# Sparse attention and a routed expert layer: the first expert's third block computed with tokens held and weights streamed

## Chip, cores and metric

One core of a Trainium2 chip runs the whole program. The metric is device time in microseconds, the median of three runs: 1031.38 us for the kernel before (1029.55 to 1036.73).

## What is computed

Eight batches of eight heads of attention over 576 tokens with head size 64, in which each query keeps its 32 largest scores. Its output is the input `x` (4608 tokens of 512 values) of a layer with eight experts: a token with `x @ w_skip > 0` goes to the one expert with the largest gate value.

```python
scores = scale * np.matmul(q, k.transpose(0, 1, 3, 2))
kth = np.partition(scores, -top_k, axis=-1)[..., -top_k:-top_k + 1]
scores = np.where(scores >= kth, scores, -1000000000.0)
...
for e in range(E):
    mask = e_idx == e
    h = np.maximum(xc[mask] @ w1[e], 0.0)
    y[mask] = gate_w[mask, None] * (h @ w2[e])
out[do_compute] = xc + y
```

## The kernel before

The attention takes the first 779 us of the span, the experts the rest. Only the expert stage matters here, and in it the passage from the first expert to the second.

Tokens are gathered by expert into blocks of 128 (`XG`, at most `NB` = 3 blocks, so `TN` = 384 tokens). A block is turned by four PE transposes into a px buffer (two of these in PSUM), ACT copies it as `XH` (the high part, line 1052), and DVE writes the remainder `XL` (line 1056). Weights are split in the same manner: ACT writes the high part (`part_hi`, line 966), DVE the remainder (`part_lo`, line 969), in four quarters per layer. Every product is then three products of high and low parts.

`up` (lines 1111 to 1118) computes 128 hidden values of all tokens of a stretch: the weights are held in the array, the tokens are streamed, 12 products into a ph buffer (three of these). ACT's relu writes the high part of the hidden values to `HH[f]` (line 1121), DVE the remainder to `HL[f]` (line 1124); f runs over `FC` = 8 groups of 128 hidden values. `down` (lines 1135 to 1141) holds 128 hidden values of a block's 128 tokens and streams 512 columns of the second layer, three products for each f and block, into py, one buffer for each block.

The first expert (e = 0) is computed while the last routing step is still running: its first two blocks (`EARLY` = 2) with ups of 224 tokens (32 to 256) and their downs, then the third block alone, once its tokens are gathered: `upping(EARLY * P, TN, ...)`, eight ups of 128 tokens. These pieces are handed to the planner `pl`, which sorts tasks on each engine by readiness and due times and writes the program order that the engines follow. In the same call the three blocks of the second expert are gathered by POOL and turned (`turning(1, j, ...)`), and the first-layer weights of the second expert are split as soon as the ups that read the old ones are done (`done`). After `pl.run()` the order is that of plain code: the downs of the third block (e = 0), with the splits of the second-layer weights (`ahead_of`) between them, then for e = 1 to 7 eight ups with relus and splits, and the downs with the splits of the next second layer and the turns of the next expert.

Weights come by transfers on SP's queue (`fetch`), tokens by indirect transfers on POOL's queue (line 1029), and sums go back by line 1042.

Of the kernel before, what the change touches and what calls it, by code (L numbers as in the profile page):

```python
# [9 lines left out]
F32 = mybir.dt.float32  # L10
# [3 lines left out]
AF = mybir.ActivationFunctionType  # L14
# [9 lines left out]
EARLY = NBLK - 1  # L24
# [19 lines left out]
def tile_kernel(ctx, tc, q, k, v, w_skip, w_gate, w1, w2, out):  # L44
    nc = tc.nc
# [4 lines left out]
    P = 128  # L50
# [9 lines left out]
    CC = DM // P  # L60
# [29 lines left out]
    identF = cp.tile([P, P], F32, name="identF")  # L90
# [180 lines left out]
    pl = Plan()  # L271
# [19 lines left out]
    for c0, n, src in ((0, E, w_gate), (E, 1, w_skip.rearrange("(f o) -> f o", o=1))):  # L291
        gates.append((GW[:, :, c0:c0 + n], src.rearrange("(c p) e -> p c e", p=P)))
        pairs = src.rearrange("(c u d) e -> u d c e", u=2, d=D)
        for u in range(2):
            c = c0 + (E + 1) * u
# [31 lines left out]
    NB = NBLK  # L327
# [615 lines left out]
    FC = F // P  # L943
    FQ = F // 4
    TN = NB * P
    WHI, WLO = [None] * 2, [None, [None] * 4]
    WRAW = [WA, [WB[:, i] for i in range(4)]]
    XG, XH, XL = [None] * 2, [None] * 2, [None] * 2
# [75 lines left out]
    room_of = lambda e: (TN,) [0] if e == 0 else ROOM[e - 1]  # L1024
# [13 lines left out]
    def finish(xg, j, ix, py):  # L1038
        scatter(summed(xg, j, py), ix)
# [23 lines left out]
    def turning(e, j, bank, due, after):  # L1063

        h = Hold(bank, 2)
        st = {}
        x = pl.add("PE", 0.47, due, lambda: st.__setitem__("v", turned(e, j, h()[:, 0:512])), after, take=h)
        x = pl.add("ACT", 0.48, due, lambda: turned_hi(e, j, st["v"]), x, give=[h])
        return pl.add("DVE", 0.6, due, lambda: turned_lo(e, j, st["v"]), x, give=[h])
# [13 lines left out]
    PARTED = []  # L1083
    FETCHED = {}
    for n in range(16):
        w, i, half = n // 8, n // 2 % 4, n % 2
        FETCHED.setdefault((w, i), []).append(pl.add("SP", 0.63, NR * NP * n // 16 - K["ld"] + K["fe"], lambda w=w, i=i, half=half: fetch(0, w, i, half),
                                                     LOADED[0, NP * n // 16], lag=5.0))
    for i in range(4):
        x = pl.add("ACT", 1.06, D0 + 1 + i, lambda i=i: part_hi(0, i), room, PENNED[NP - 1], FETCHED[0, i])  # L1090
        PARTED.append(pl.add("DVE", 1.22, D0 + 1 + i, lambda i=i: part_lo(0, i), x))
    x = pl.add("DVE", 0.3, D0, lambda: to_index(IDX[0], LS, EB), ROUTED[0])
    y = pl.add("POOL", 1.6, D0, lambda: nc.gpsimd.memset(XG[0], 0.0), room)
    XT = []
    for j in range(EARLY):
        g = pl.add("POOL", 1.1, D0, lambda j=j: gather(XG[0], j, ix(0, j), N - S), x, y, STORED[B - 2], [STORES[p] for p in range(NP - H // 2)], lag=3.0)
# [5 lines left out]
    mp = ms.enter_context(tc.tile_pool(name="mp", bufs=1, reuse_waits="tile"))  # L1102
# [8 lines left out]
    def up(e, f, ph, u, w):  # L1111

        xh, xl = XH[e % 2], XL[e % 2]
        h1, l1 = (a[0][f // 2].rearrange("p (c f) -> p c f", c=CC)[:, :, f % 2 * P:(f % 2 + 1) * P] for a in (WHI, WLO))
        for c in range(CC):
            nc.tensor.matmul(ph[:, u:w], h1[:, c], xh[:, c, u:w], start=(c == 0), stop=False)  # L1116
            nc.tensor.matmul(ph[:, u:w], h1[:, c], xl[:, c, u:w], start=False, stop=False)  # L1117
            nc.tensor.matmul(ph[:, u:w], l1[:, c], xh[:, c, u:w], start=False, stop=(c == CC - 1))  # L1118
# [11 lines left out]
    D1 = D0 + 10  # L1130
# [12 lines left out]
    def upping(u, w, due, after):  # L1143
        r = []
        for f in range(FC):
            h = Hold(PH, 2)
            x = pl.add("PE", 12 * max((w - u) / 2400 + 0.013, 0.107), due + 0.4 * f, lambda f=f, h=h: up(0, f, h(), u, w), PARTED[f // 2], after, take=h)
            y = pl.add("ACT", 0.17 + (w - u) / 1200, due + 0.4 * f, lambda f=f, h=h: relu_hi(f, h.t, u, w), x, give=[h])
            r.append((x, pl.add("DVE", 0.16 + (w - u) / 960, due + 0.4 * f, lambda f=f, h=h: relu_lo(f, h.t, u, w), y, give=[h])))
        return r  # L1150
# [16 lines left out]
    x = pl.add("DVE", 0.35, D1, places, ROUTED[0])  # L1167
    pl.add("DVE", 2.6, D1 + 2, lambda: sort_experts(IDXF, IDX[1]), x)
    g = pl.add("POOL", 1.1, D1, lambda: gather(XG[0], NB - 1, ix(0, NB - 1)), x, STORED[B - 1], STORES[NP - 1], lag=3.0)
    done = upping(EARLY * P, TN, D1 + 12, turning(0, NB - 1, PX, D1 + 8, g))  # L1170
    for j in range(NB):
        g = pl.add("POOL", 1.1, D1 + 1, lambda j=j: gather(XG[1], j, ix(1, j)), x, STORED[B - 1], STORES[NP - 1], lag=3.0)
        turning(1, j, PX, D1 + 12.1 + 0.8 * j, g)
# [91 lines left out]
    check = checks()  # L1265
    for j in range(EARLY):
        finish(XG[0], j, ix(0, j), PY0[j])
    for e in range(E):
        for f in range(FC) if e else ():
            ph = ps_g.tile([P, 512], F32, name="ph", bufs=3)  # L1270
            up(e, f, ph, 0, room_of(e))
            relu_hi(f, ph, 0, room_of(e))
            relu_lo(f, ph, 0, room_of(e))
            ahead_of(e, 0, f)
            if e > 1:
                next(check, None)
        PY = [ps_g.tile([P, 512], F32, name=f"py{j}", bufs=1) for j in range(NB)] if e else PY0
        ots = []
        if e + 1 < E:
            for f in range(FC):  # L1280
                for j in range(blocks_of(e)) if e else (NB - 1,):
                    down(f, j, PY[j])
                    if f == FC - 1:
                        ots.append((summed(XG[e % 2], j, PY[j]), ix(e, j)))
                ahead_of(e, 1, f)
                if e > 1:
                    next(check, None)
                if e and f % 2 and f // 2 < blocks_of(e + 1):
                    turn_x(e + 1, f // 2)
        else:  # L1290

            for j in range(blocks_of(e)):
                for f in range(FC):
                    down(f, j, PY[j])
                finish(XG[e % 2], j, ix(e, j), PY[j])
        if e + 2 < E:
            for j in range(blocks_of(e + 2)):
                gather(XG[e % 2], j, ix(e + 2, j))
        for x in ots:
            scatter(*x)  # L1300
# [210 lines left out]
```

## Time and profile before

| | us |
|---|---|
| median of 3 runs | 1031.38 |
| lowest, highest | 1029.55, 1036.73 |
| the profiled execution | 1031.82 |
| its span, first to last instruction | 1030.0 |
| PE busy | 986.7 (96%) |
| DVE busy | 896.6 (87%) |
| ACT busy | 836.3 (81%) |
| mean granted clock of PE | 0.989 |

The busy shares are means over two stages: in the attention DVE, ACT and POOL are all near 9 tenths, in the last quarter of the span they are mostly between 1 and 7, while PE stands at 9 in nearly every slice. The rows below are of the stretches around the change. A row of a timeline reads: start, time, engine, line, operation, output from inputs, shapes, how many, and in brackets the idle time before it and what ended it. A product's time holds its latency, so two products that follow one another are best read by the distance of their starts.

### The profile page before, as it was taken

What the parts mean: (1) busy time and instruction counts of PE and PEld (TensorE: products, weight loads), DVE (VectorE), ACT (ScalarE), POOL (GpSimd) and SP (SyncE); (2) the same over time, 40 slices, a digit from 0 to 9 for tenths busy, and PEclk for the clock granted to TensorE, in tenths of its full rate; (3) what the DMA queues carried; (4) which work ended last, traced back from release to release, by engine and by line L of the source; (5) the groups of instructions that cost most, each with busy time, mean ns of one, the idle gap of its engine ahead of it and who ended that gap; (6) DMA issues with size and microseconds to landing.
All of it is one profiled execution on the core that took longest, in us unless ns stands there. A gap on an engine that the chain in (4) does not pass through costs nothing.

```text
span 1030.0 us, 38832 instructions
## 1 busy us (share of the span) xinstructions
PE 986.7 (96%) x14632; PEld 700.4 (68%) x14632; DVE 896.6 (87%) x4986; ACT 836.3 (81%) x1485; POOL 706.3 (69%) x864
## 2 busy tenths in 40 slices
PE   8499999999999999999999999999999999999996
PEld 4156666666666666666666565666678889988995
DVE  6989999999999999999999999999986746765661
ACT  6799999999999999999999998999983544433540
POOL 3988899888888888988988988799961212211210
PEclk9799999999999999999999999999999999999998
DMA  5333334343443334434333333333226465554610
GB/s 126 62 87 77 87 76 98 88 103 91 100 97 77 87 90 102 99 73 114 91 88 76 87 82 93 85 86 77 48 50 206 155 215 174 175 157 158 217 66 21
DMA packets 215493, 106.64 MB, mean 104 GB/s; under 512 B 149512, under 2 KB 200712, under 8 KB 215296
## 3 DMA queue, kind: packets, MB, share of 16 engines
q1 hardware_dynamic: 210736, 94.30, 36.0%
q0 software_dynamic: 3360, 9.47, 2.7%
q8 instruction: 117, 1.92, 0.8%
q14 instruction: 80, 0.66, 0.2%
q10 hardware_dynamic: 1200, 0.30, 0.1%
HBM read 76.93 MB, written 24.53 MB: 98 GB/s over the span
## 4 chain that ended last, share of the span: by engine, by line
PE 67%; DVE 22%; ACT 5%; POOL 3%; issue 2%; DMA 1%; POOLq 0%; ACTq 0%
PE r L621 10%; PE r L769 9%; DVE cand L692 8%; DVE cl L721 5%; PE pt L852 5%; PE pa L852 4%; PE ph L1116 4%; PE py L1139 4%; PE ph L1117 4%; PE ph L1118 4%; PE py L1141 4%; PE py L1140 4%; DVE cand L700 3%; PE r L760 3%; DVE cl L698 3%
## 5 line engine op out<-in xcount | busy, mean ns | idle before, releaser
L708 POOL TENSOR_TENSOR xw<-XC,r 128x576 f32<-128x576 f32 x288 | 366.2, 1284 | 49.6 <-ACT r L705 28.7
L692 DVE MAX8 cand<-XC 128x8 f32<-128x82 f32 (+1 forms) x2016 | 364.4, 229 | 9.2 <-ACT XC L649 9.1
L705 ACT ACTIVATE r<-XC,cl 128x576 bf16<-128x576 f32 x288 | 224.9, 785 | 11.5 <-DVE cl L698 8.4
L721 DVE MAX8 cl<-xw 128x8 f32<-128x585 f32 x288 | 215.6, 756 | 3.1 <-POOL xw L712 1.5
L621 PE MATMUL r<-TT 64*64 64x512 f32 (+1 forms) x1280 | 190.3, 416 | 0.8 <-ACT XC L630 0.7
L716 POOL TENSOR_SCALAR PEN<-XC,cl 128x576 bf16<-128x576 f32 x94 | 162.7, 1731 | 24.2 <-DVE cand L700 12.3
L769 PE MATMUL r<-TT 64*128 64x512 f32 (+1 forms) x528 | 148.8, 641 | 12.0 <-ACT XC L651 12.0
L621 PE MATMUL r<-TS 64*64 64x512 f32 (+1 forms) x1024 | 154.3, 416 | 1.4 <-DMA TS<-TT 1.4
L718 ACT ACTIVATE PEN<-XC,cl 128x576 bf16<-128x576 f32 x194 | 150.1, 788 | 3.7 <-DVE cl L721 3.7
L698 DVE MAX8 cl<-cand 128x8 f32<-128x56 f32 (+2 forms) x864 | 151.9, 182 | 0.2
L802 ACT ACTIVATE PTM<-r,tops 128x1024 f32<-128x1024 f32 x124 | 137.6, 1121 | 6.3 <-PE r L760 5.9
L649 ACT ACTIVATE XC<-r 128x1024 f32<-128x1024 f32 x128 | 132.5, 1038 | 4.3 <-PE r L621 4.1
L760 PEld LDWEIGHTS <-PEN 64*128 64x128 bf16 (+1 forms) x2880 | 71.0, 100 | 73.8 <-issue 67.0
L712 POOL TENSOR_SCALAR xw<-wo,CN 128x9 f32<-128x9 f32 x288 | 100.5, 349 | 26.3
L700 DVE MATCH_REPLACE8 cand<-cl,cand 128x14 f32<-128x14 f32 (+1 forms) x576 | 96.0, 169 | 0.0
L1029 POOL DMA_INDIRECT xg<-xd,idx x21 | 23.7, 1127 | 101.8 <-DVE ot L1035 88.1
L1116 PE MATMUL ph<-xh,hi 128*128 128x224 f32 (+4 forms) x288 | 84.7, 294 | 0.3 <-DVE xl L1056 0.3
L966 ACT ACTIVATE hi<-wb 128x1024 fp32r<-128x1024 f32 x32 | 33.7, 1059 | 63.1 <-PE py L1141 62.8
L1118 PE MATMUL ph<-xh,lo 128*128 128x224 f32 (+4 forms) x288 | 84.5, 293 | 0.0
L1117 PE MATMUL ph<-xl,hi 128*128 128x224 f32 (+4 forms) x288 | 84.4, 293 | 0.0
L1042 POOL DMA_INDIRECT out_dram<-ot,idx x21 | 22.4, 1067 | 90.1 <-DVE ot L1035 47.5
L852 PE MATMUL pt<-VG,PTM 128*64 128x65 f32 x2240 | 81.1, 224 | 1.7 <-DVE xb L865 1.2
(263 smaller groups left out, 2047.7 us busy)
## 6 DMA issues: line engine op xcount, KB each, us to landing
raw<-in_moe_w_dram SPq DMA_DIRECT2D x28, 512.0 KB, 3.8
wb<-in_moe_w_dram SPq DMA_DIRECT2D x28, 512.0 KB, 3.6
TS<-TT SPq DMA_DIRECT2D x64, 144.0 KB, 2.7
out_dram<-xd SPq DMA_DIRECT2D x32, 288.0 KB, 3.1
raw<-in_k_dram SPq DMA_DIRECT2D x64, 128.0 KB, 3.1
VG<-in_v_dram SPq DMA_DIRECT2D x64, 128.0 KB, 2.6
xd<-xb SPq DMA_DIRECT2D x32, 256.0 KB, 2.9
raw<-in_q_dram SPq DMA_DIRECT2D x62, 128.0 KB, 2.7
```

The costliest lines, as they stand in the source:

```text
L621: nc.tensor.matmul(o[hs_(h)], q_, (ts[src, u:w] if y else tt[src, 0, u:w]), start=True, stop=True)
L649: nc.scalar.activation(xc[:, t:u + 1:u - t, 0:MAIN], h2.t.rearrange("p (y c) -> p y c", y=2), AF.Copy)
L692: nc.vector.max(C_[:, c], xc[:, CH[c]:CH[c + 1]])
L698: nc.vector.max(L[:, 4 * r:4 * r + 8], c)
L705: nc.scalar.activation(rr_, xc, AF.Sign, bias=CL[p % 2][:, t, 23:24], scale=-ODD, accum_out=CN[:, s:s + 1])
L708: nc.gpsimd.tensor_tensor(xw[:, 0:S], xc, rr_, op=OP.mult)
L716: nc.gpsimd.tensor_scalar(pen, xc, WN[p % 2][:, t, 7:8], None, op0=OP.is_lt)
L718: nc.scalar.activation(pen, xc, AF.Relu, bias=WN[p % 2][:, t, 7:8], scale=-1.0)
L721: nc.vector.max(WN[p % 2][:, t], xw)
L769: nc.tensor.matmul(rb[:, 512 * h + u:512 * h + w], tt[hs_(h), 0, REM + P * kc:REM + P * (kc + 1)], tt[hs_(h), 1, REM + u:REM + w], start=T ...
L802: nc.scalar.activation(o_.rearrange("p h c -> p (h c)"), i_, AF.Exp, bias=nb, scale=scale)
L852: nc.tensor.matmul(h.t[hs_(t % 2), VW * (t // 2):VW * (t // 2 + 1)], w, vg[:, a, kc], start=(kc == 0 and t < 2), stop=(kc == NM), skip_gro ...
```

## The change

For the third block of the first expert the roles of tokens and weights are exchanged. `up_tokens(i, ph)` holds the block's 128 tokens and streams 256 columns of first-layer weights; two quarters fill one ph buffer with 128 tokens x 512 hidden values, in 24 products, and i = 0, 1 covers all 1024. The result lies the other way round, so ACT writes its relu to `HT[i]` (two new buffers), four PE transposes turn it back into a px buffer (`turn_hidden`), and eight small copies on ACT and differences on DVE (`hidden`, 128 columns each) write `HH[f]` and `HL[f]`. The tasks wait for all four quarters of the split weights, and both splits of a half stand behind that half's product (`done`). In the planner the name `x` on which the gathers of the second expert wait is now the last copy of hidden values.

In the plain code the first two ups of the second expert are issued ahead of the first expert's third-block downs; their relus stay where they were.

```diff
-    done = upping(EARLY * P, TN, D1 + 12, turning(0, NB - 1, PX, D1 + 8, g))
+    HT = [mp.tile([P, 512], F32, name=f"ht{i}") for i in range(2)]
+
+    def up_tokens(i, ph):
+
+        js = slice(EARLY * P, TN)
+        for q in range(2):
+            h1, l1 = (a[0][2 * i + q].rearrange("p (c f) -> p c f", c=CC) for a in (WHI, WLO))
+            o = ph[:, q * FQ:(q + 1) * FQ]
+            for c in range(CC):
+                nc.tensor.matmul(o, XH[0][:, c, js], h1[:, c], start=(c == 0), stop=False)
+                nc.tensor.matmul(o, XL[0][:, c, js], h1[:, c], start=False, stop=False)
+                nc.tensor.matmul(o, XH[0][:, c, js], l1[:, c], start=False, stop=(c == CC - 1))
+
+    def turn_hidden(i, px):
+        for j in range(FC // 2):
+            nc.tensor.transpose(px[:, j * P:(j + 1) * P], HT[i][:, j * P:(j + 1) * P], identF)
+
+    def hidden(i, px, lo):
+        for j in range(FC // 2):
+            f, o = i * FC // 2 + j, px[:, j * P:(j + 1) * P]
+            if lo:
+                nc.vector.tensor_sub(HL[f][:, EARLY * P:TN], o, HH[f][:, EARLY * P:TN])
+            else:
+                nc.scalar.activation(HH[f][:, EARLY * P:TN], o, AF.Copy)
+
+    tx = turning(0, NB - 1, PX, D1 + 8, g)
+    done = []
+    for i in range(2):
+        h, h2 = Hold(PH, 1), Hold(PX, 2)
+        x = pl.add("PE", 2.9, D1 + 12 + i, lambda i=i, h=h: up_tokens(i, h()), PARTED, tx, take=h)
+        done += [[x]] * (FC // 2)
+        x = pl.add("ACT", 0.48, D1 + 12 + i, lambda i=i, h=h: nc.scalar.activation(HT[i], h.t, AF.Relu), x, give=[h])
+        x = pl.add("PE", 0.475, D1 + 12.5 + i, lambda i=i, h2=h2: turn_hidden(i, h2()), x, take=h2)
+        x = pl.add("ACT", 0.63, D1 + 12.5 + i, lambda i=i, h2=h2: hidden(i, h2.t, False), x, give=[h2])
+        pl.add("DVE", 0.8, D1 + 12.5 + i, lambda i=i, h2=h2: hidden(i, h2.t, True), x, give=[h2])
     for j in range(NB):
         g = pl.add("POOL", 1.1, D1 + 1, lambda j=j: gather(XG[1], j, ix(1, j)), x, STORED[B - 1], STORES[NP - 1], lag=3.0)
         turning(1, j, PX, D1 + 12.1 + 0.8 * j, g)
...
+    begun = []
+    for f in range(2):
+        begun.append(ps_g.tile([P, 512], F32, name="ph", bufs=3))
+        up(1, f, begun[f], 0, room_of(1))
     for e in range(E):
         for f in range(FC) if e else ():
-            ph = ps_g.tile([P, 512], F32, name="ph", bufs=3)
-            up(e, f, ph, 0, room_of(e))
+            if begun:
+                ph = begun.pop(0)
+            else:
+                ph = ps_g.tile([P, 512], F32, name="ph", bufs=3)
+                up(e, f, ph, 0, room_of(e))
             relu_hi(f, ph, 0, room_of(e))
```

PE of the changed kernel behind the last products of the third block (`ht` are the two turned-round halves, `xg_15460` the second expert's gathered blocks, `xh_15461` their turned high parts):

```order
L1181 MATMUL ph<-lo_15056,xh_15062 128x256
L1185 MATMUL px<-identF,ht_15483 128x128 x4
L1185 MATMUL px<-identF,ht_15484 128x128 x4
L1048 MATMUL px<-identF,xg_15460 128x128 x12
L1116 MATMUL ph<-xh_15461,hi_15049 128x336
```

In the kernel before, the three groups of four transposes of `xg_15460` stood singly between the ups of 128 tokens; now all twelve stand behind the turned halves, and the second expert's first up follows them.

ACT in the kernel before, from the copy of the third block (`xh_15062`) on; `xh_15461` is the second expert's, `hi` are split weights, `hh` hidden values:

```order
L1052 ACTIVATE xh_15062<-px 128x4x128
L1052 ACTIVATE xh_15461<-px 128x4x128
L1121 ACTIVATE hh_15444<-ph 128x128
L1121 ACTIVATE hh_15445<-ph 128x128
L966 ACTIVATE hi_15049<-raw_15440 128x1024
L1121 ACTIVATE hh_15446<-ph 128x128
L1052 ACTIVATE xh_15461<-px 128x4x128
L1121 ACTIVATE hh_15447<-ph 128x128
L966 ACTIVATE hi_15050<-raw_15441 128x1024
```

And ACT of the changed kernel from the relu of the second half on:

```order
L1201 ACTIVATE ht_15484<-ph 128x512
L1193 ACTIVATE hh_15444<-px 128x128
L1193 ACTIVATE hh_15445<-px 128x128
L1193 ACTIVATE hh_15446<-px 128x128
L1193 ACTIVATE hh_15447<-px 128x128
L966 ACTIVATE hi_15051<-raw_15442 128x1024
L1193 ACTIVATE hh_15448<-px 128x128
L1193 ACTIVATE hh_15449<-px 128x128
L1193 ACTIVATE hh_15450<-px 128x128
L1193 ACTIVATE hh_15451<-px 128x128
L966 ACTIVATE hi_15052<-raw_15443 128x1024
L1052 ACTIVATE xh_15461<-px 128x4x128 x3
```

The copies of the second expert's three blocks have moved from between the relus to the end of the piece.

DVE of the changed kernel at the same place (`lo` are the remainders of split weights, `hl` those of hidden values, `xl_15462` those of the second expert's blocks):

```order
L969 TENSOR_TENSOR lo_15055<-raw_15442,hi_15051 128x1024
L1191 TENSOR_TENSOR hl_15456<-px,hh_15448 128x128
L1191 TENSOR_TENSOR hl_15457<-px,hh_15449 128x128
L1191 TENSOR_TENSOR hl_15458<-px,hh_15450 128x128
L1191 TENSOR_TENSOR hl_15459<-px,hh_15451 128x128
L969 TENSOR_TENSOR lo_15056<-raw_15443,hi_15052 128x1024
L1056 TENSOR_TENSOR xl_15462<-px,xh_15461 128x4x128 x3
```

Here too the second expert's blocks stand behind the last split, where they stood singly between the splits before.

## Rows read from the trace of the kernel before

**Rows 1.** Waits of PE from 770 us on: us in total, times, longest.

```profile
PE px L1048 <- DMA xg<-xd,idx: 0.9, 1, 0.9
PE r L1048 <- DMA xg<-xd,idx: 0.9, 2, 0.5
PE ph L1116 <- DVE xl L1056: 0.3, 1, 0.3
```

**Rows 2.** Timeline of PE, third block, its downs, next expert's ups.

```profile
802.86 0.63 PE L1048 MATMUL px<-identF,xg 128*128 128x128 f32 x4 [0.94 <-DMA xg<-xd,idx]
...
803.50 0.27 PE L1118 MATMUL ph<-xh,lo 128*128 128x128 f32 x1
...
807.18 0.28 PE L1118 MATMUL ph<-xh,lo 128*128 128x128 f32 x1
807.29 0.63 PE L1048 MATMUL px<-identF,xg 128*128 128x128 f32 x4
807.67 0.31 PE L1116 MATMUL ph<-xh,hi 128*128 128x128 f32 x1
...
814.81 0.45 PE L1139 MATMUL py<-hi,hh 128*128 128x512 f32 x1
...
820.48 0.31 PE L1116 MATMUL ph<-xh,hi 128*128 128x336 f32 x1
...
835.30 0.32 PE L1118 MATMUL ph<-xh,lo 128*128 128x336 f32 x1
```

**Rows 3.** Timeline of PE, ups of a later expert with 256 tokens.

```profile
951.05 0.28 PE L1118 MATMUL ph<-xh,lo 128*128 128x256 f32 x1
...
952.70 0.28 PE L1117 MATMUL ph<-xl,hi 128*128 128x256 f32 x1
```

**Rows 4.** Timeline of ACT beside the third block.

```profile
801.95 0.60 ACT L1052 ACTIVATE xh<-px 128x512 fp32r<-128x512 f32 x1 [10.17 <-PE px L1048]
...
806.15 0.28 ACT L1121 ACTIVATE hh<-ph 128x128 fp32r<-128x128 f32 x1 [1.06 <-PE ph L1118]
806.33 1.05 ACT L966 ACTIVATE hi<-raw 128x1024 fp32r<-128x1024 f32 x1
```

**Rows 5.** Timeline of DVE beside the third block and the next ups.

```profile
802.58 0.69 DVE L1056 TENSOR_TENSOR xl<-px,xh 128x512 fp32r<-128x512 f32 x1 [2.01 <-ACT xh L1052]
...
807.41 1.23 DVE L969 TENSOR_TENSOR lo<-raw,hi 128x1024 fp32r<-128x1024 f32 x1 [0.66 <-ACT hi L966]
808.55 0.28 DVE L1124 SCALAR_TENSOR_TENSOR hl<-ph,hh 128x128 fp32r<-128x128 f32 x1
808.75 0.68 DVE L1056 TENSOR_TENSOR xl<-px,xh 128x512 fp32r<-128x512 f32 x1
...
823.93 0.50 DVE L1124 SCALAR_TENSOR_TENSOR hl<-ph,hh 128x336 fp32r<-128x336 f32 x1
```

**Rows 6.** Stretches: length, then busy us of PE, PEld, DVE, ACT, POOL, clock, DMA.

```profile
68.00:71.50 3.50, 2.42 (x21) 1.53 (x22) 3.22 (x19) 3.50 (x10) 2.92 (x4) 1.00 0.62 152
71.50:75.00 3.50, 3.50 (x24) 1.49 (x26) 3.50 (x26) 2.48 (x3) 3.23 (x5) 0.51 0.47 93
45.60:51.00 5.40, 5.37 (x42) 2.66 (x44) 5.40 (x42) 3.78 (x6) 5.07 (x7) 0.50 0.00 0
774.50:778.00 3.50, 2.64 (x27) 2.20 (x23) 1.46 (x4) 1.85 (x5) 1.94 (x11) 1.00 0.61 166
```

**Rows 7.** Timeline of PE in the attention, before, under and after the low clock.

```profile
69.13 1.06 PE L533 MATMUL pt<-GW,XTT 128*128 128x9 f32 x8 [1.08 <-ACT XTT L526]
...
71.37 1.94 PE L769 MATMUL r<-TT 64*128 64x512 f32 x4
...
75.41 1.11 PE L769 MATMUL r<-TT 64*128 64x512 f32 x4
```

**Rows 8.** Timeline of POOL, first gather for the expert after next.

```profile
823.60 1.34 POOL L1029 DMA_INDIRECT xg<-xd,idx  x1 [0.30 <-issue]
```

**Rows 9.** Timeline of PE, first turned block of the expert after next.

```profile
839.66 0.60 PE L1048 MATMUL px<-identF,xg 128*128 128x128 f32 x4
```

## Prediction

> **What bounds the kernel now.** I read first the waits of PE from 770 us to the end [rows 1]. In the expert stage PE has three kinds of wait, 2.1 us in all, and the last of them, 0.94 us for a gathered block, ends at 802.86, in front of the third block [rows 1, 2]. From there to the end of its work it never waits. So in this stage a microsecond taken from PE's own work, with nothing put in its place, is a microsecond of the kernel, and a microsecond of new waiting is one too, since no later slack of PE takes it up. Next I read the third block in PE's timeline [rows 2]: 96 products of 128 tokens between 802.86 and 814.81, with the three turns of the next expert's blocks among them, then 24 downs (814.81 to 820.48), then the next expert's ups. ACT's and DVE's rows of the same stretch [rows 4, 5] show that beside each pair of ups they do relus, a split of weights and a turned block: the small work is spread under PE. Last I read the granted clock around the places where PE is not fed steadily [rows 6, 7].
>
> **PE's own work.** Products follow one another faster than each lasts, so I go by their spacing. Of 128 columns: 803.50 to 807.18 is 33 steps, 0.1115 us each [rows 2]. Of 256 columns: 951.05 to 952.70 is 14 steps, 0.118 each [rows 3]. Removed: 96 x 0.1115 = 10.70. Added: 48 x 0.118 = 5.66, and 8 transposes at 0.38 for four (807.29 to 807.67) [rows 2], 0.76. PE's work falls by 4.3 us. With tokens stationary the shape of an added product is the same as that of the 256-column rows (128x128 held, 256 streamed), but no row shows the roles exchanged; bounds are 0.1115 below (the 128-column row) and 0.156 above (336 columns, 820.48 to 835.30 in 95 steps [rows 2]), that is 5.4 to 7.5 us for the 48. I take 0.118.
>
> **What is moved, and what hides it no more.** In the kernel before, the three turns of the next expert stand between the ups on PE; in the changed order all twelve transposes stand in one piece behind both products and both turns of the hidden values, and on ACT and DVE the copies xh and xl of these turns stand behind all four splits and all eight small copies of each engine. PE cannot go past them: the next expert's first up, which stands next, needs all three turned blocks (336 columns), and the downs, whose inputs are done earlier, are queued behind it. The turned blocks share two px buffers with the turned hidden values, so the third of them waits until xl of the first is done.
>
> I lay this out from the row of xl at 802.58 [rows 5], which ends at 803.27 and which the change leaves where it is. A hand-over takes 0.03 (xh ends at 802.55, xl starts at 802.58 [rows 4, 5]), and an engine starts its next piece 0.10 before the last one's end (806.15 + 0.28 against 806.33 [rows 4]), so small copies follow at 0.18 on ACT, 0.20 on DVE (808.55 to 808.75), a split on DVE takes 1.14 (807.41 to 808.55) [rows 5].
> - PE: both products from 803.3, 5.66, last value at 809.1.
> - ACT: relu of the second half, 0.60 (the row of xh, as wide): 809.1 to 809.75. The first half's relu and the first two splits lie under PE's second product, so they cost nothing.
> - ACT: four small copies, 0.72, then the third split, 1.05: to 811.4.
> - DVE: third lo, 1.14, four small differences, 0.80, fourth lo, 1.14: to 814.5. ACT is ahead here (fourth hi ends at 813.1).
> - DVE: xl of the first turned block, 0.69: 815.2. Only now is the px buffer free for the third.
> - PE four transposes 0.66, ACT xh 0.63, DVE xl 0.72, each with its hand-over: 817.25.
> So the next expert's first up runs from about 817.2, its first product alone earlier. The two ups take 24 x 0.156 = 3.74, the downs 5.67 (as before), and the third up starts at 826.6. Before, it started at 820.48 + 3.74 = 824.22 [rows 2]. The 4.3 us of saved work have become 2.4 us of loss.
>
> **A second wait.** The relus of the two early ups stand on ACT and DVE behind the splits of the second layer's weights, and the last of these waits for the last down. From the last down's end (0.16 behind the third up's start) it takes 1.05 for hi, 1.14 for lo, 0.50 for the first hl [rows 4, 5], with hand-overs about 2.8 us until one of the three ph buffers is free. The third up covers 1.87 of that, the fourth waits 1.1. Before, this was covered by the first two ups, which ran behind the downs. Lower bound 0 (a third buffer free earlier), upper 2.8. Loss so far: 3.5 us.
>
> **No further waits.** No transfer is added. The gathers for the expert after next wait on POOL for the third block's sum, so for the last down, which ends 6 us later than before; the first was issued at 823.60 [rows 8] and its block is turned at 839.66 [rows 9], which itself moves by 3.5 or more, so more than ten microseconds of slack stay. On SP the fetches of the weights after next stand behind the splits that free their buffers: the first lo ended at 808.64 [rows 5] and now ends at 809.1, the fourth now ends at 814.6, before the last product that it waited for in the kernel before.
>
> **The clock.** Between 809.0 and 817.2 PE now gets five groups of four transposes with gaps up to 1.6 us. In the trace a stretch like that cost the clock: from 68.0 to 71.5 PE was busy 2.42 of 3.5 us, with ten products of few columns and no gap over 1.08 us, and at 71.5 the granted clock fell to 0.51 until 75.0 (1.2 in place of 2.4 GHz), though PE was by then fully busy [rows 6, 7]. From 774.5 to 778.0, with 13 transposes and 2.64 us busy, it held [rows 6]. The changed stretch is lighter than either: in its last 5 us two groups, 1.3 us busy. I take it that the clock falls there. The cost: the same four products took 1.94 at the low clock and 1.11 at the full one [rows 7], so 43% of the time spent low is lost. How long it stays low after PE resumes is bounded by 3.4 us (71.5 to 75.0, PE busy already) and 5.4 us (45.6 to 51.0, out of a pause [rows 6]); the second is nearer, as PE comes out of waiting: 5.4 x 0.43 = 2.3 us. With the first it would be 1.5, and without a fall 0.
>
> The Trainium skill ("TensorE: Matmul & The Clock Gate", the table under "Why this matters for your kernels") warns of idle gaps between bursts of matmuls, longer ones than the gaps here; by that rule the clock would hold and the sum would be 3.5. The row at 71.5 differs: the clock fell there with no such gap. The same page's "Part 4: PE-mode transpose" says that a transpose does not count as work for the clock in the way of other products; by that the groups of four would not break the pause, the clock would fall, and the sum would be the one below; the row that held with 13 transposes speaks against taking it strictly.
>
> **Sum.** 3.5 + 2.3 = 5.8 us on the profiled execution's 1031.82 (span 1030.0), 1037.6. That execution stands 0.44 above the median of the runs, 1031.38, so for the median I say 1037.2.
>
> **Rivals.**
> - The clock holds, as in the row at 774.5: 3.5 us alone, 1034.9 for the median. For it: five groups of transposes, no long gap. Against it: 71.5. Chance 0.20.
> - The clock stays low for another stretch, or falls early so that the turns run low too: another 3.4 x 0.43 = 1.5 us and some tenths, 1039 or a little more. For it: no row shows how early in such a stretch it falls. Against it: in both rows the low clock ended within 5.4 us of steady work. Chance 0.13.
> - The saved work counts: the turns of the next expert finish under PE's work and the waits don't arise, 1031.38 - 4.3 = 1027.1. It decides at the start of the next expert's first up: 814.8 is the break-even, 813.7 with the second wait. Against it: DVE alone has two splits, eight differences and three xl behind its second lo (ending near 810.3), 2.28 + 1.60 + 1.9 = 5.8 us, which ends at 816 even if it never waits. For it only: these pieces could be shorter than their rows. Chance 0.05.
> - The forecast, 0.62, with its own range of 1035.5 to 1038.5 (low clock 3.4 to 5.4 us, second wait 0.5 to 1.5).
>
> **How the numbers follow.** The likeliest gives 1037.2. Down from it the range must take in the clock that holds (1034.9) less a microsecond of run-to-run difference and of a shorter second wait; up, the longer low clock: 1033.5 to 1040.0, which leaves out the gain and part of the second rival. About 1%, 10.3 us, is what a measurement of this kernel tells from no change. All cases but outliers lie inside it: slower by over 1% would take low clock over some 16 us from one pause (0.04), faster by over 1% no case here gives (0.01); within 1%: 0.95.
>
> **What the changed profile would show.** Right: PE's products of 256 columns at 0.118 spacing up to about 809; then waits of PE for DVE in front of the turned blocks and of the next expert's first up, which starts near 817; downs right behind the two early ups; one wait of about 1 us for hl in front of the fourth up; a granted clock of 0.5 over some microseconds around 816 to 822. Wrong: no wait of PE in front of the next expert's first up; a spacing far from 0.118; a clock of 1.00 throughout; or later waits of PE for the moved gathers.

## The result and the profile after

| | before | after |
|---|---|---|
| median (6 runs each, taken together) | 1030.86 us | 1037.05 us |
| lowest, highest | 1029.55, 1036.73 | 1035.85, 1038.46 |
| span of the profiled execution | 1030.0 | 1034.1 |
| PE busy | 986.7 (96%) | 985.3 (95%) |
| mean granted clock of PE | 0.989 | 0.986 |

The ratio is 1.0054, with a 95% interval of 1.0032 to 1.0077: slower by half a per cent, less than the 1% that was called no change. The medians differ by 6.2 us. The predicted 1037.2 us is 0.15 above the median, and that closeness is partly luck: it was built on the 1031.38 of the first three runs, 0.5 above the median of all six, and on a sum of 5.8, 0.4 below the measured difference. Two of the runs below, the new block alone and the gathers' wait, each had one execution that was far slower (1101.91 and 1209.63 us) and is left out of their medians and ratios.

The profiled execution of after began its third block 2.3 us earlier than that of before, because its attention happened to end earlier. Spans of single executions can't be compared to a microsecond, so from here on I use the **stage time**: from the start of the third block's xl (DVE, line 1056) to the start of the last down product (line 1141). Before it was 802.58 to 1019.50, 216.9 us; after it was 800.25 to 1023.60, 223.35 us, that is 6.4 more. Each stage time is from one execution. From the third up of the second expert to the end of the stage the six executions without a wait there agree to 0.4 us (195.07 to 195.49), and in every run the change of the stage time and the change by the ratio differ by less than 0.9 us.

The waits of PE from 770 us on in after, in us, times, longest (before: [rows 1]):

```profile
PE px L1048 <- DVE hl L1191: 2.4, 2, 1.4
PE ph L1116 <- DVE hl L1124: 1.4, 1, 1.4
PE px L1048 <- DVE xl L1056: 1.1, 1, 1.1
PE ph L1179 <- issue: 0.7, 1, 0.7
PE ph L1116 <- ACT xh L1052: 0.7, 1, 0.7
```

Every one of them lies between the start of the third block and the fourth up of the next expert; from 831 us to the end there is none. The wait of 0.94 for a gathered block [rows 1, 2] is gone, since the turned blocks now stand later. In its place the third block waits for its own xh and xl: its third product starts 0.98 behind the start of xl (801.23 less 800.25), before 0.92 [rows 2, 5].

PE's timeline of after (before: [rows 2]). Lines 1179 to 1181 are the three products of `up_tokens`, 1185 is the turning back, 1048 a turned block of the second expert, 1116 to 1118 are its ups, 1139 to 1141 downs:

```profile
800.27 0.38 PE L1179 MATMUL ph<-hi,xh 128*128 128x256 f32 x1 [0.69 <-issue]
800.99 0.39 PE L1180 MATMUL ph<-hi,xl 128*128 128x256 f32 x1 [0.34 <-DVE xl L1056]
801.23 0.28 PE L1181 MATMUL ph<-lo,xh 128*128 128x256 f32 x1
...
806.57 0.28 PE L1181 MATMUL ph<-lo,xh 128*128 128x256 f32 x1
806.68 0.60 PE L1185 MATMUL px<-identF,ht 128*128 128x128 f32 x4
807.53 0.66 PE L1185 MATMUL px<-identF,ht 128*128 128x128 f32 x4 [0.25 <-ACT ht L1201]
809.13 0.66 PE L1048 MATMUL px<-identF,xg 128*128 128x128 f32 x4 [0.94 <-DVE hl L1191]
811.20 0.66 PE L1048 MATMUL px<-identF,xg 128*128 128x128 f32 x4 [1.41 <-DVE hl L1191]
812.93 0.80 PE L1048 MATMUL px<-identF,xg 128*128 128x128 f32 x4 [1.08 <-DVE xl L1056]
814.42 0.65 PE L1116 MATMUL ph<-xh,hi 128*128 128x336 f32 x1 [0.69 <-ACT xh L1052]
815.15 0.65 PE L1117 MATMUL ph<-xl,hi 128*128 128x336 f32 x1
...
819.79 0.48 PE L1118 MATMUL ph<-xh,lo 128*128 128x336 f32 x1
820.07 0.36 PE L1116 MATMUL ph<-xh,hi 128*128 128x336 f32 x1
...
821.04 0.39 PE L1139 MATMUL py<-hi,hh 128*128 128x512 f32 x1
...
826.65 0.32 PE L1116 MATMUL ph<-xh,hi 128*128 128x336 f32 x1
...
828.36 0.32 PE L1118 MATMUL ph<-xh,lo 128*128 128x336 f32 x1
830.08 0.42 PE L1116 MATMUL ph<-xh,hi 128*128 128x336 f32 x1 [1.40 <-DVE hl L1124]
```

The 48 products run at a spacing of 0.119 (801.23 to 806.57 is 45 steps). After that five groups of four transposes stand in single file, and each but the first waits. The two early ups run at 0.28 from product to product up to 820.07 and at 0.155 behind it: the first is the low clock, the second the full one.

What PE waits for is seen on DVE (before: [rows 5]):

```profile
808.19 0.88 DVE L1191 TENSOR_TENSOR hl<-px,hh 128x128 fp32r<-128x128 f32 x4 [0.22 <-ACT hh L1193]
809.12 1.22 DVE L969 TENSOR_TENSOR lo<-raw,hi 128x1024 fp32r<-128x1024 f32 x1
810.27 0.88 DVE L1191 TENSOR_TENSOR hl<-px,hh 128x128 fp32r<-128x128 f32 x4
811.06 1.22 DVE L969 TENSOR_TENSOR lo<-raw,hi 128x1024 fp32r<-128x1024 f32 x1
812.19 1.28 DVE L1056 TENSOR_TENSOR xl<-px,xh 128x512 fp32r<-128x512 f32 x2
```

From 808.19 to 813.47 DVE is idle for no more than 0.05 us: differences of the hidden values, splits of weights and xl by turns. Each group of differences and each xl lets one px buffer go; the splits between them only take time. PE, which has two px buffers for five groups of transposes, moves at DVE's pace.

The stretches of after: length, busy us of PE, PEld, DVE, ACT, POOL, granted clock, DMA share, GB/s (the attention's rows are [rows 6]):

```profile
808.00:813.00 5.00, 1.57 (x11) 0.91 (x10) 4.76 (x12) 3.79 (x9) 0.00 (x0) 1.00 0.86 275
813.00:813.50 0.50, 0.50 (x4) 0.35 (x4) 0.47 (x1) 0.00 (x0) 0.00 (x0) 0.81 0.61 211
813.50:820.00 6.50, 5.74 (x20) 5.14 (x19) 2.01 (x3) 0.60 (x1) 1.47 (x2) 0.50 0.37 126
820.00:821.00 1.00, 1.00 (x7) 1.00 (x7) 0.00 (x0) 0.00 (x0) 0.70 (x2) 0.93 0.00 0
```

In 808 to 813 PE is busy 1.57 of 5 us. At 813.31 (0.81 in half a microsecond is 0.19 low) the clock falls from 2.4 to 1.2 GHz, and at 820.14 (0.93 in one is 0.14 low) it is back: 6.83 us. The fall doesn't seem to belong to the profiled execution alone: over the span the mean granted clock was 0.984 to 0.986 in all six executions of after, and 0.987 to 0.989 in the six of the run with fillers below. The kernel before has mostly 0.987 to 0.989, but single executions down to 0.983.

### The profile page after: what moved, and what is told of

Same layout as the page of the kernel before. It is cut to its first block, busy times and chain, and to the rows that moved or that the text cites. A ratio compares the mean times of both kernels' runs of the same rounds, so it can differ in the third digit from the quotient of the medians.

```text
span 1034.1 us, 38753 instructions
## 1 busy us (share of the span) xinstructions
PE 985.3 (95%) x14592; PEld 697.5 (67%) x14592; DVE 896.2 (87%) x4986; ACT 835.9 (81%) x1487; POOL 705.5 (68%) x864
## 4 chain that ended last, share of the span: by engine, by line
PE 66%; DVE 25%; POOL 4%; ACT 3%; issue 2%; DMA 0%; SPq 0%; POOLq 0%; ACTq 0%; DVEq 0%
PE r L621 10%; DVE cand L692 9%; PE r L769 9%; DVE cl L721 6%; PE pt L852 5%; PE pa L852 4%; PE py L1139 4%; PE py L1141 4%; PE py L1140 4%; PE ph L1117 3%; PE ph L1116 3%; PE ph L1118 3%; DVE cand L700 3%; PE r L760 3%; DVE cl L698 3%; POOL xw L708 2%
## 5 line engine op out<-in xcount | busy, mean ns | idle before, releaser
L649 ACT ACTIVATE XC<-r 128x1024 f32<-128x1024 f32 x128 | 132.1, 1035 | 4.3 <-PE r L621 4.0
L712 POOL TENSOR_SCALAR xw<-wo,CN 128x9 f32<-128x9 f32 x288 | 100.1, 348 | 26.3
L621 PEld LDWEIGHTS r<-TT 64*64 64x64 f32 x1280 | 55.9, 133 | 36.4 <-issue 25.4
L1116 PE MATMUL ph<-xh,hi 128*128 128x224 f32 (+3 forms) x256 | 77.1, 301 | 2.1 <-DVE hl L1124 1.4
L969 DVE TENSOR_TENSOR wa<-wb,hi 128x1024 fp32r<-128x1024 f32 x32 | 39.1, 1223 | 45.7 <-ACT hi L966 45.7
```

The lines of the kernel that those rows point to most:

```text
L621: nc.tensor.matmul(o[hs_(h)], q_, (ts[src, u:w] if y else tt[src, 0, u:w]), start=True, stop=True)
L649: nc.scalar.activation(xc[:, t:u + 1:u - t, 0:MAIN], h2.t.rearrange("p (y c) -> p y c", y=2), AF.Copy)
```

## The experiments

Three things could make up the 6.4 us: the chain behind the third block, the wait before the fourth up, and the clock. In the first four runs each takes away one part or one suspected cost. Expectations use the stage time.

**The third block's new form alone.** The early ups are left out; the downs stand behind the turned blocks, as in the kernel before.

```diff
     begun = []
-    for f in range(2):
-        begun.append(ps_g.tile([P, 512], F32, name="ph", bufs=3))
-        up(1, f, begun[f], 0, room_of(1))
```

> The changed kernel without its second half: the third block with tokens held and its values turned back, but the second expert's first two ups stand behind the downs again, as in the kernel before. I count in stage time, from the start of xl of the third block to the start of the last product: 216.9 us before (802.58 to 1019.50), 223.4 changed (800.25 to 1023.60). My theory (the loss is the chain of small copies and splits ahead of the second expert's turned blocks, a wait for a ph buffer, and the low clock): the downs need not wait for xh and xl of the last turned block, so PE resumes about 1.3 us earlier, and the wait of 1.4 us in front of the fourth up is gone; the clock still falls. Stage about 220.5, so 3 to 4 us over the kernel before. Rival (the early ups are cover for the turned block, and without them PE waits longer): stage 223.4 or more. Rival (the exchange of roles itself is slow on PE): spacing of the 256-column products well over 0.118.

1033.96 us against 1031.84 before, ratio 1.0022 (1.0012 to 1.0031). Stage 802.61 to 1022.30, 219.7: 2.8 more than before and 3.7 less than after, and 0.8 less than expected. PE's timeline of this run:

```profile
811.49 0.66 PE L1048 MATMUL px<-identF,xg 128*128 128x128 f32 x4 [0.94 <-DVE hl L1191]
813.55 1.11 PE L1048 MATMUL px<-identF,xg 128*128 128x128 f32 x4 [1.41 <-DVE hl L1191]
```

The waits for px buffers are the same as in after (0.94, 1.41), so they come with the new block and not with the early ups. The clock fell here too, from 812.59 to 819.42. The wait for the last xh and the wait before the fourth up are not there: the downs need neither. The new block alone already turns the 4 us of saved work into a loss.

**The early ups alone.** The third block of before, with the two ups ahead of its downs.

```diff
+    begun = []
+    for f in range(2):
+        begun.append(ps_g.tile([P, 512], F32, name="ph", bufs=3))
+        up(1, f, begun[f], 0, room_of(1))
...
```

> The kernel before with only the second half of the change: the second expert's first two ups ahead of the third block's downs, the third block as it was. My theory: the turned blocks are ready then, so PE does not wait in front of the early ups and the clock stays at 1.00; what is left is the one wait in front of the fourth up, for hl behind the last split of the second layer, about 1.4 us. Stage 218.3, 1.4 us over the kernel before. Rival (the early ups are harmless or help, all of the loss is the turning back): stage 216.9, no wait. Rival (the early ups bring the larger part of the loss): stage over 220.

1033.47 us, ratio 1.0010 (1.0000 to 1.0019). Stage 802.95 to 1021.48, 218.5, 1.6 more than before. Behind the third block PE waits once:

```profile
827.97 0.42 PE L1116 MATMUL ph<-xh,hi 128*128 128x336 f32 x1 [1.40 <-DVE hl L1124]
```

It is the second wait of the prediction, with the same 1.40 as in after; the interval of the ratio only touches 1, so this run is read by the wait and the stage. It costs 1.6 and not 1.4, because the idle time is counted from the end of a product that lasts 0.32, while the next could have started 0.155 behind its start. The clock stays at 1.00 from 802.95 to 830 us: this one gap doesn't bring it down.

**The clock held up by fillers.** After, with 15 products of 512 columns in the stretches in which PE waits; they compute nothing that is read.

```diff
+    def fill(n):
+        for _ in range(n):
+            nc.tensor.matmul(PY0[NB - 1], XH[0][:, 0, 0:P], WHI[1][0][:, 0:512], start=True, stop=True)
...
+    FILL.update({("h", 0): 1, ("h", 1): 3, (1, 0): 5, (1, 1): 4, (1, 2): 2})
```

> The changed kernel with 15 products of 512 columns more on PE, written into the py buffer of the third block before its downs clear it, so into nothing that is read: 1 and 3 behind the two turns of hidden values, 5, 4 and 2 behind the three turned blocks of the second expert. At 0.234 us each they fit into PE's waits there (0.25, 0.94, 1.41, 1.08, 1.4). My theory that the low clock is a part of the loss of its own: the clock stays at 1.00, the two early ups run at a spacing of 0.156 in place of 0.28, and the stage falls by 2.3 us to about 221.1, with the waits as they were. Rival (the low clock costs nothing because what follows it waits anyway, or fillers cost what they bring): stage 223.4 or more. If the clock falls in spite of the fillers: stage about 223.4, and the row tells nothing on the price.

1035.44 us, ratio 1.0035 (1.0023 to 1.0047). Stage 803.32 to 1024.27, 220.95, which is 2.4 less than after, with 15 products more. The stretches of this run, and rows of PE to which the part on the prediction comes back (lines are 9 further on than in after: 1126 is the second product of the first early up, 1148 the first down, 1125 the start of the third up):

```profile
808.00:814.00 6.00, 5.70 (x37) 4.35 (x36) 5.11 (x11) 5.67 (x14) 0.00 (x0) 1.00 0.44 135
814.00:820.00 6.00, 5.12 (x28) 3.93 (x29) 4.50 (x7) 1.40 (x3) 1.03 (x1) 1.00 0.68 217
```

```profile
818.01 0.42 PE L1126 MATMUL ph<-xl,hi 128*128 128x336 f32 x1 [0.31 <-DVE xl L1056]
...
821.70 0.40 PE L1148 MATMUL py<-hi,hh 128*128 128x512 f32 x1
...
827.31 0.31 PE L1125 MATMUL ph<-xh,hi 128*128 128x336 f32 x1
```

The clock stays at 1.00 when PE is kept busy. So the light stretch made it fall, and the fall cost 2.4 us. (Waits of 0.22 to 0.31 us are left ahead of the first two turned blocks and of the first two products of the first up, so the fillers hold up none of these.)

**The relus of the early ups ahead of the splits.** They stand behind the first two downs (f = 0 and 1), in front of the first split of the second layer, instead of behind all downs and all splits. `early` are the ph buffers of the two ups.

```diff
+    early = list(begun)
...
-            relu_hi(f, ph, 0, room_of(e))
-            relu_lo(f, ph, 0, room_of(e))
...
+                if e == 0 and f == 1:
+                    for i in range(2):
+                        relu_hi(i, early[i], 0, room_of(1))
+                        relu_lo(i, early[i], 0, room_of(1))
```

> The changed kernel with the relus of the two early ups (hh and hl) moved ahead: behind the second pair of downs, in front of the splits of the second-layer weights, in place of behind all four. My theory of the second wait: the ph buffer is then free long before the fourth up wants it, the wait of 1.4 us for hl is gone, nothing else moves up in its place, stage 221.9. Rival (the wait moves on to the splits, since ACT and DVE have the same work to do and the sixth up or the next downs wait for it): stage 223.0 to 223.8 with a new wait of PE for DVE behind the fourth up.

1036.97 us, ratio 1.0045 (1.0031 to 1.0058). Stage 803.52 to 1024.83, 221.3: 2.0 less than after. The wait before the fourth up is gone and nothing takes its place, so it came from the relus' place behind the splits, as predicted. 1.6 of the 2.0 is that wait. Of the other 0.4, 0.16 lies ahead of the third up (26.24 us behind the third block's xl in place of 26.40), where the low clock fell and ended 0.65 earlier; the rest is no more than the executions differ by. In total times after, the run with fillers and this one are not told apart (their intervals overlap); that verdict rests on the stage times and on the waits.

Take the clock's 2.4 and the wait's 1.6 from the 6.4, and 2.4 us are left: the chain, less what the new block saves PE. The next runs ask why that chain is there at all: because of the block's copies and splits themselves, or because of where the turned blocks stand.

**The gathers wait for the sorted places again.** The change had given the name `x` to the last hidden copy, and the planner's tasks of the second expert's gathers, written below it, took that as what they wait for. One name puts the old dependence back:

```diff
-    x = pl.add("DVE", 0.35, D1, places, ROUTED[0])
+    x = placed = pl.add("DVE", 0.35, D1, places, ROUTED[0])
...
-        g = pl.add("POOL", 1.1, D1 + 1, lambda j=j: gather(XG[1], j, ix(1, j)), x, ...)
+        g = pl.add("POOL", 1.1, D1 + 1, lambda j=j: gather(XG[1], j, ix(1, j)), placed, ...)
```

> The changed kernel, where the gathers of the second expert's tokens wait in the planner's tasks for the sorted places again, and no longer for the last hidden copy of the third block (a name that the change had overwritten). Of the second expert's three turned blocks, one then stands on PE between the first expert's last turn and the first product of 256 columns, one between the two products, and one behind the first turn of hidden values. Stage time is from the start of the third block's xl to the start of the last product (216.9 us before, 223.4 after). Theory (the turns stand too late, behind all of the third block, and this starves PE and costs it its clock): PE's waits for the turned blocks mostly go, one wait of about 1.5 us stays ahead of the second turn of hidden values, the clock stays at 1.00, the wait of 1.4 us before the fourth up stays: stage about 215.9, a time of about 1030. Rival (the loss is in the third block's copies and splits themselves, wherever the turns stand): waits of 3 us or more again and a low clock again, stage 222 or more, a time of about 1036.

1030.08 us against 1031.21 before, ratio 0.9988 (0.9979 to 0.9998). Stage 801.95 to 1018.09, 216.1, 7.2 less than after from one name; the clock's 2.4 is part of that. PE's timeline of this run:

```profile
805.53 0.60 PE L1048 MATMUL px<-identF,xg 128*128 128x128 f32 x4
...
808.82 0.60 PE L1185 MATMUL px<-identF,ht 128*128 128x128 f32 x4
809.25 0.60 PE L1048 MATMUL px<-identF,xg 128*128 128x128 f32 x4
811.36 0.63 PE L1185 MATMUL px<-identF,ht 128*128 128x128 f32 x4 [1.50 <-DVE hl L1191]
...
824.55 0.42 PE L1116 MATMUL ph<-xh,hi 128*128 128x336 f32 x1 [1.40 <-DVE hl L1124]
```

The turned block at 805.53 stands between the two products, another is ahead of the first, and only one remains behind. One px wait of 1.50 is left, then the 1.40 before the fourth up. The clock stays at 1.00, though PE is busy only 0.64 of 2 us here:

```profile
810.00:812.00 2.00, 0.64 (x6) 0.67 (x7) 1.82 (x7) 2.00 (x5) 0.00 (x0) 1.00 0.89 281
```

So most of the loss came from where the turned blocks stand. Of the block's own copies and splits this px wait of 1.50 is what is left.

**The same with the early relus.** Both edits above together.

> The kernel with the gathers' earlier wait (the run e5), and the relus of the two early ups ahead of the splits of the second layer's weights. Theory (the wait before the fourth up comes only from these relus standing behind the splits): that wait goes and nothing takes its place: stage about 214.5, 1.4 less than the run with the gathers' wait alone, a time of about 1028.5. Rival (ACT and DVE are too full there, and the splits, now later, hold up the next expert's weights or another up): no gain over the run with the gathers' wait alone.

1029.48 us, ratio 0.9983 (0.9973 to 0.9992). Stage 802.58 to 1017.08, 214.5, 1.6 less. The wait before the fourth up is gone; the px wait of 1.50 stays.

**The new block in time, without the early ups.**

> The third block with tokens stationary and the gathers' earlier wait, but without the early ups: the downs stand right behind the second turn of hidden values, as in the kernel before. Stage time as in the other runs (216.9 us before). Theory (with the turns in time the early ups hide nothing that the downs would not hide, and only bring the wait of 1.4 us before the fourth up): the wait of 1.5 us ahead of the second turn of hidden values stays, no wait before the fourth up, stage about 214.6, the same as the run with the gathers' wait and the early relus, a time of about 1029. Rival (the downs come too early for the hidden values of the second half, which the early ups covered): a new wait of a down for hl of about 1 us or more, stage 215.6 or more.

1028.90 us against 1031.63, ratio 0.9967 (0.9954 to 0.9980). Stage 802.71 to 1017.04, 214.3, within 0.2 of the run with early relus. The waits of PE in this run begin with

```profile
PE px L1185 <- DVE hl L1191: 1.5, 1, 1.5
PE px L1048 <- DMA xg<-xd,idx: 1.0, 1, 1.0
```

and no down waits. Once the turned blocks stand in time, the early ups cover nothing in this order that the downs would not.

**The early ups with early relus, on the block of before.**

> The kernel before with the early ups alone, and their relus ahead of the splits of the second layer's weights (behind the first two pairs of downs). Theory (the early ups cost only by the wait before the fourth up, and give nothing): that wait is gone, clock 1.00, stage 216.9 and the time of the kernel before, within 0.1%. Rival 1 (the early ups are a gain once their relus are in time): stage under 216. Rival 2 (ACT and DVE are too full behind the third block): stage 217.8 or more, with another wait of PE.

1032.48 us, ratio 1.0005 (0.9994 to 1.0016). Stage 802.50 to 1019.43, 216.9, the time of before. In this form the early ups neither cost nor bring anything.

**All of it in an order written by hand.** The same work as after, with the gathers' earlier wait and the early relus of the runs above, and with the turned blocks and splits spread between the pieces that PE runs. `half` is the product of one half of the hidden values, `back` its turning back with the small copies and differences, `turn_x` a turned block, `part` a split:

```diff
+    turn_x(1, 0)
+    half(0)
+    relu_half(0)
+    turn_x(1, 1)
+    turn_x(1, 2)
+    half(1)
+    part(0, 0)
+    relu_half(1)
+    back(0)
+    begun = [ps_g.tile([P, 512], F32, name="ph", bufs=3)]
+    up(1, 0, begun[0], 0, room_of(1))
+    part(0, 1)
+    back(1)
+    begun.append(ps_g.tile([P, 512], F32, name="ph", bufs=3))
+    up(1, 1, begun[1], 0, room_of(1))
+    part(0, 2)
+    part(0, 3)
```

> The same work as the changed kernel with the third block, the second expert's turns, the splits and the early ups in an order written by hand: a turned block, first product, two turned blocks, second product, split, first turn of hidden values, first early up, split, second turn of hidden values, second early up, two splits, downs; relus of the early ups behind the first two pairs of downs. Theory (the 4.3 us of PE's work are really saved, and all of the loss is waits and clock that the order makes): no wait of PE over 0.3 us from the third block to the fourth up, clock 1.00, stage about 212.7, 4.2 less than before, a time of about 1027. Rival (products of 256 moving columns in this block, or the turning back, cost PE more than their spacing says): stage 215 or more though the waits are gone.

1028.26 us against 1031.21, ratio 0.9969 (0.9958 to 0.9981). Stage 803.66 to 1016.61, 212.95, 4.0 less than before. PE's timeline of this run:

```profile
810.94 0.60 PE L1185 MATMUL px<-identF,ht 128*128 128x128 f32 x4
811.29 0.40 PE L1116 MATMUL ph<-xh,hi 128*128 128x336 f32 x1
811.53 0.32 PE L1117 MATMUL ph<-xl,hi 128*128 128x336 f32 x1
...
813.22 0.60 PE L1185 MATMUL px<-identF,ht 128*128 128x128 f32 x4
813.57 0.40 PE L1116 MATMUL ph<-xh,hi 128*128 128x336 f32 x1
```

Behind the 0.89 for the first gathered block, which was there before, the list of PE's waits has nothing up to the end. An early up stands between the two turns back while ACT and DVE copy the first, and the px wait of 1.50 is gone: here the early ups seem to have a use. That is read from the rows; no run has this order without them. PE's busy time in the stage shows what the new block really saves. Before (its two pieces together):

```profile
sum 216.92, PE 216.65 PEld 195.10 DVE 130.14 ACT 90.80 POOL 38.32; mean PE 108.32 PEld 97.55 DVE 65.07 ACT 45.40 POOL 19.16
```

and in this order:

```profile
sum 212.95, PE 212.70 PEld 190.84 DVE 129.56 ACT 90.70 POOL 39.23; mean PE 106.35 PEld 95.42 DVE 64.78 ACT 45.35 POOL 19.61
```

216.65 less 212.70 is 3.95 us, and the stage is shorter by the same amount. By the medians this version and the one without early ups are 0.3% faster than the kernel before and 0.8% faster than after; the two are not told apart.

## Why the prediction was right

The forecast had the right path: work saved on PE, lost again to a chain on ACT and DVE, then a wait for a ph buffer and a fall of the clock. Three of the terms have runs of their own. PE's work is from the hand order: -4.0. The wait before the fourth up is from the early ups alone: +1.6. The clock is from the run with fillers: +2.4. The chain is what is then left between fillers and hand order, 220.95 less 212.95 less 1.6, so that the column adds up to 6.4 by its making and is no check. A check that doesn't go by these totals: with fillers, so without the low clock, the third up of the second expert starts 23.99 us behind the third block's xl (827.31 less 803.32), in the kernel before 21.64 (824.22 less 802.58). That is 2.35 more, where the prediction has 2.4 for the chain less the saved work.

| term | predicted | measured |
|---|---|---|
| PE's work | -4.3 | -4.0 |
| chain behind the third block | +6.7 (so that -4.3 becomes +2.4) | +6.4 |
| wait before the fourth up | +1.1 | +1.6 |
| low clock | +2.3 | +2.4 |
| sum | +5.8 | +6.4 |

- **PE's own work.** The spacing was taken as 0.118 from rows of another stage with the operands in the other roles [rows 3], and is 0.119. The saving is 0.3 smaller than the sum. The first product behind a group of transposes stands 0.24 ahead of its successor in place of 0.155 (811.29 to 811.53, in the hand order), which is part of that.
- **The chain.** It holds row by row. Counted from the start of the third block's xl, the prediction has the third split on ACT end at 8.8, DVE reach the first xl at 11.9, and the third up at 26.3 with the low clock. The rows of after have 8.8 (808.00 and 1.09, less 800.25), 11.9 (812.19) and 26.4 (826.65). The next expert's first up was put at 14.6; its first product is at 14.2 and its second, which needs xl, at 14.9.
- **The second wait.** Its mechanism and place are right and shown by two runs; the size was 1.1 and is 1.6 in the stage (830.08 less 826.65, less the 1.87 of the third up). The step let the last split's remainder (wa) start as soon as ACT's high part is written. DVE's timeline of after shows what stands ahead of it (`wa` is the remainder of a second-layer weight):

```profile
826.58 1.23 DVE L969 TENSOR_TENSOR wa<-wb,hi 128x1024 fp32r<-128x1024 f32 x1 [0.18 <-ACT hi L966]
827.73 0.74 DVE L1035 SCALAR_TENSOR_TENSOR ot<-py,xg 128x512 f32<-128x512 f32 x1
828.39 1.22 DVE L969 TENSOR_TENSOR wa<-wb,hi 128x1024 fp32r<-128x1024 f32 x1
829.52 0.92 DVE L1124 SCALAR_TENSOR_TENSOR hl<-ph,hh 128x336 fp32r<-128x336 f32 x2
```

The high part ended at 827.96, wa started at 828.39: the third block's sum (line 1035), which the last down releases at the same time, stands between two splits. The step left this out, though the kernel before has the same order: in its trace the third block's sum starts at 822.14 and the last wa at 822.80.
- **The clock.** It fell where it was predicted, and from the light stretch, as the fillers show. The prediction took 5.4 us at the low clock from where PE is fed again [rows 6]. Here that is 5.7 us, from the first up's first product (814.42) to 820.14; in the run of the new block alone it was 3.4, from the first down at 816.05 to 819.42. So the length fits partly by luck: what was alike in the three falls is the whole low stretch, 6.8 us, and how much of it is left when PE comes back differs. The price can be read from the rows. The 23 products from 815.15 to the first down at 821.04 take 5.89 us in after, and with fillers 3.69 (818.01 to 821.70). That is 2.2 more, and the third turned block takes 0.14 more (0.80 for 0.66): 2.3 of the 2.4. Between 813.73 and 815.15 PE waits for xh and xl, and the low clock costs nothing. The Trainium skill ("TensorE: Matmul & The Clock Gate", the table under "Why this matters for your kernels") asks, against drops in the middle of a kernel, for no long idle gaps between bursts of matmuls. The longest gap ahead of the fall was 1.41 us, shorter than those it warns of, so that this rule alone would have kept the clock and given about 1034.9. The trace decides against it here.
- **No further waits.** Right in its outcome: PE waits for nothing from 831 us to the end. Its reason is wrong in part. It has the gathers for the expert after next wait for the third block's sum, but only the third of them does. The first and the third on POOL in after:

```profile
820.86 1.05 POOL L1029 DMA_INDIRECT xg<-xd,idx  x1 [0.30 <-issue]
...
828.74 1.74 POOL L1029 DMA_INDIRECT xg<-xd,idx  x1 [5.51 <-DVE ot L1035]
```

The first is issued earlier than in the kernel before (823.60 there [rows 8]), the third later (828.74 in place of 826.57). The first of these blocks is turned at 843.75 in place of 839.66 [rows 9], still without a wait.
- **What the prediction didn't see** is why the turned blocks stand so late. It took the order as it was and costed it well, and the section on the change mentions the name on which the gathers wait; but it gave no word to that dependence as the cause. It is worth 7.2 of the stage's microseconds, more than all of the loss, the clock's 2.4 among them. The rival in which the saved work counts was rightly improbable for this order, and is what the same work gives in another.

## What to carry to other kernels

Work saved on the engine that bounds the kernel is only a gain if what it used to cover is still covered: lay out the small work of the other engines behind the shortened piece, buffer by buffer, and ask what stands in single file. Where a planner writes the order, read which task each later task depends on by name; a variable that is used again can move a dozen instructions without any line of theirs being changed. A low clock comes on top of the waits that cause it, so the cheapest repair is to have the waits go, not to fill them.

## What the runs showed of the hardware

- Three runs had a fall of the clock in this stage, and its low stretch lasted 6.83 us in after (813.31 to 820.14), 6.83 in the run of the new block alone (812.59 to 819.42) and 6.82 in the run with early relus (815.94 to 822.76), though PE came back to steady work at different distances from the fall. In the attention of before one low stretch was 3.4 us long. The 5.4 us of [rows 6] are only the last part of another, behind a pause of PE of 12.03 us: the clock stood at 0.50 in that pause too (42.00 to 45.60).
- The moment of the fall does not follow from PE's rows of the third block: counted from the third block's xl it came 13.1, 10.0 and 12.4 us later in these three, although their PE rows, counted so, agree to 0.1 us until the earliest of the falls. What sets it isn't shown.
- One gap of 1.40 or 1.50 us left the clock at 1.00 (early ups alone; gathers' wait), and so did 0.64 us of PE's work in 2 us; four gaps of 0.25 to 1.41 us between groups of transposes, with 1.57 us of work in 5 (after), went ahead of a fall. Whether it always falls in such a stretch isn't shown: each run has one profiled execution, and the mean clocks of the others only speak for it.
